# Expert pages of a top-1 MoE on one NeuronCore: token rows fetched as quarter rows and turned by VectorE instead of TensorE

## The chip, the cores and the metric

One core of a Trainium2 chip runs one launch of the kernel. The metric is the device time of that launch in microseconds (us), as the median of several runs. The engines are named as in the profile: PE (TensorE, matmuls and transposes), DVE (VectorE), ACT (ScalarE), POOL (GpSimd, here also the issuer of indirect DMAs) and SP (SyncE, the issuer of the plain DMAs).

## The reference

Sink-and-window attention (4 batches, 8 heads, 768 positions, head dimension 64), its output laid out as 3072 tokens of 512, then an FFN with `h * cos(h)`, then a mixture of 8 experts of which each token uses one. The change lies in the last part:

```python
def _moe2_ref(x, modality_id, w_gate, modality_bias, w1, w2):
    logits = x @ w_gate + modality_bias[modality_id]
    e_idx = np.argmax(logits, axis=1)
    probs = np.exp(logits - logits.max(-1, keepdims=True))
    probs /= probs.sum(-1, keepdims=True) + 1e-09
    gate_w = probs[np.arange(N), e_idx]
    for e in range(E):
        mask = e_idx == e
        h = np.maximum(x[mask] @ w1[e], 0.0)      # 512 -> 1024
        out[mask] = gate_w[mask, None] * (h @ w2[e])  # 1024 -> 512
    return out
```

Everything is float32. `x` here is the output of the FFN, one row of 512 for each token.

## The kernel before, in words

**Precision.** Each factor of a product is split into a high and a low part (`split`, L1096; `xh`, `xl`), and a product is three matmuls: high by high, high by low, low by high.

**Stages.** Attention and the FFN run first, woven into each other, in tiles of 384 tokens. `route_tile` computes a tile's gates and writes its rows to the DRAM scratch `y_scr`, 513 floats for each token: 512 of the row and the gate. It also counts where each token goes, and the table `inv` (128 by 192) ends with the token numbers in the order of the experts, a column for each half page.

**Pages.** The expert stage works on pages of 256 tokens of one expert. A page T passes through these steps:

- `gather_rows(T)` (L1116): six DVE operations of 128 by 2 turn two columns of `inv` into row numbers for the gather (`m_idg`) and for the scatter (`m_ids`). Both have four slots, T mod 4.
- `gather_go(T)` (L1128): two indirect DMAs on POOL's queue (L1131), each 128 rows of 513 floats, into `m_yg[T % 2]`. The token lies on the partition, so the row must be turned before it can be a factor of a product over the 512.
- `prelude(T)` (L1135): eight PE transposes of 128 by 128 (L1143) into PSUM, in two groups of four; after each group one copy on ACT (`xh`, L1144) and one subtraction on DVE (`xl`, by the helper at L149).
- `first_product` (L1147): 96 matmuls; ACT (L1154) and DVE (L146) make the two parts of `hT`.
- `second_product(T, h)`, for each half h: 48 matmuls, the copy `m_ot` on ACT with the gate as its scale (L1185), and the scatter of 128 rows to `out` on POOL's queue (L1188).

**Order.** From page 2 on a manual schedule holds: every engine runs its instructions in the order in which the code issues them. A full page T goes through the `If` branch of `run` (L1337): `first_product(T)`; then `ahead`: the load of the next expert's weights where the expert changes, `prelude(T+1)`, `second_product(T, 0)` with the splits of the next expert's first weights between its steps; then `gather_rows(T+2)`; then `second_product(T, 1)` with `gather_go(T+2)` between its copy and its scatter. A page of at most 128 tokens goes through the `Else` branch: it has half the work, and `gather_rows(T+2)` comes before `prelude(T+1)` there. Page 0 and the `prelude` of page 1 lie ahead of the manual schedule, woven into the end of the FFN.

**This input.** The run has pages 0 to 13. Pages 6 and 13 are half pages; the expert changes at page 6 and again at page 7, so that page 6 is the only page of its expert. In the profile page 2 starts at 850.80, page 6 at 946.1 and page 7 at 960.4 us.

Of the kernel before, what the change touches and what calls it, by code (L numbers as in the profile page):

```python
# [11 lines left out]
F32 = DT.float32  # L12
# [8 lines left out]
P = 128  # L21
# [41 lines left out]
def kernel(  # L63
# [634 lines left out]
    def ffn_tile_gen(ypool_of):  # L698
# [24 lines left out]
        for c in range(n_all + LAG):  # L723
# [28 lines left out]
            if c == n_all + LAG - 3:  # L752
                for r_ in routes:
                    for _ in r_:
                        pass
                routes.clear()
                ysb[NTILE] = [ypool_of().tile([P, YC], F32, name="yt", bufs=NQ) for _ in range(NQ)]
                for t in range(NQ):
                    SP.dma_start(out=ysb[NTILE][t][:, 0:DM], in_=yp_scr[t])
            i, f = seq[c - LAG] if c >= LAG else (0, -1)  # L760
            if f == span(i)[1] - 1:
# [6 lines left out]
                elif i == NTILE:  # L768
                    for t in range(NQ):
                        yt = ysb[i][t][:, 0:DM]  # L770
                        tt(DVE, yt, yps[i][t], yt, ALU.add)
                    ysb[0] = ysb.pop(NTILE)
                    routes.append(route_tile(0, ypool_of()))
                else:
                    ysb[i] = []
                    for t in range(NQ):
                        yt = ypool_of().tile([P, YC], F32, name="yt", bufs=NQ)
                        ACT.activation(out=yt[:, 0:DM], in_=yps[i][t], func=AF.Copy)
                        ysb[i].append(yt)
                    routes.append(route_tile(i, ypool_of()))  # L780
# [3 lines left out]
    def route_tile(i, yp):  # L784
# [284 lines left out]
    rw2 = fin.tile([P, KE, DM], F32, name="rw2")  # L1069
    m_yg = [[fin.tile([P, YC], F32, name=f"m_yg{i}{h}") for h in range(2)] for i in range(2)]  # L1070
    m_ix = [fin.tile([P, 2], F32, name=f"m_ix{i}") for i in range(4)]
# [17 lines left out]
    def load_raw(e, cond=None):  # L1089
        kw = {} if cond is None else dict(cond=cond, cond_hint=False)  # L1090
        for c in range(KD):
            SP.dma_start(out=rw1[:, c, :], in_=w1[ds(e, 1), c * P:(c + 1) * P, :].rearrange("o p f -> p (o f)"), **kw)
        for c in range(0, KE, 2):
            SP.dma_start(out=rw2[:, c:c + 2, :], in_=w2[ds(e, 1), c * P:(c + 2) * P, :].rearrange("o (c p) d -> p (o c) d", p=P), **kw)
# [16 lines left out]

    def gather(T, col, rows=NT):
        gather_rows(T, col)
        gather_go(T, rows)

# [11 lines left out]

    def gather_go(T, rows=NT):  # L1128
        idg = m_idg[T % 4]
        for h in range(2):  # L1130
            POOL.indirect_dma_start(out=m_yg[T % 2][h], out_offset=None, in_=y_scr[0:rows, :],  # L1131
                                    in_offset=bass.IndirectOffsetOnAxis(ap=idg[:, h:h + 1], axis=0),
                                    bounds_check=rows - 1, oob_is_err=False)

    def prelude(T, banks):  # L1135
# [40 lines left out]
    def second_product(T, h, yp, between=None, behind=None):  # L1176
        i = T % 2
        s = slice(h * P, (h + 1) * P)
        for f in range(KE):
# [3 lines left out]
            if between is not None:  # L1183
                between(f)
        ACT.activation(out=m_ot[h], in_=yp, func=AF.Copy, scale=m_yg[i][h][:, DM:YC])  # L1185
        if behind is not None:
# [12 lines left out]
    def lead():  # L1199
# [8 lines left out]
        load_raw(e0)  # L1208
        gather(0, e0 * NTI, NT - 2 * HALF)
        return e0  # L1210
# [14 lines left out]

    gather(1, e0 * NTI + 2)

# [113 lines left out]
    def run(T):  # L1341
# [39 lines left out]
        with tc.If(flags[T, "full"] > 0, preferred_fallthrough_block=True, label=f"full{T}" if T > 1 else None) as full:  # L1381
# [62 lines left out]
```

## Time and profile before

| | us |
|---|---|
| median of 3 runs | 1129.12 (1128.71 to 1129.29) |
| the profiled execution | 1130.26 |
| span of its profile | 1128.5 |
| busy: PE, PE weight loads | 1085.8 (96%), 917.2 (81%) |
| busy: DVE, ACT, POOL | 700.3 (62%), 607.9 (54%), 247.3 (22%) |

The span runs from the first to the last recorded instruction; the execution's own time has 1.76 us around it. A share of busy time is a mean over stages that differ: in the expert stage, from about 827 us on, DVE and ACT have little to do, and POOL issues DMAs alone. The chain that ended last is 82% PE, 6% DVE, 4% DMA and 3% ACT.

### The profile page before, as it was taken

The numbers are of one execution on the slowest core, as the hardware profiler recorded it, in microseconds if no ns is written. First come the engines' busy times: TensorE is split into PE (matmuls) and PEld (weight loads), VectorE is DVE, ScalarE is ACT, GpSimd is POOL, SyncE is SP. The second block draws the span as 40 slices with busy tenths as digits, with TensorE's granted clock in tenths as the row PEclk, the third lists the DMA queues.
The fourth block names the chain that finished last, engine by engine and source line by source line (L and its number), as shares of the span: only waits on it lengthen the run. The fifth ranks groups of instructions, "written<-read, shape, count | busy, mean of one in ns | idle before, by whom it ended". The sixth has DMA issues, their size and how long they took to land.

```text
span 1128.5 us, 20688 instructions
## 1 busy us (share of the span) xinstructions
PE 1085.8 (96%) x6432; PEld 917.2 (81%) x6432; DVE 700.3 (62%) x2186; ACT 607.9 (54%) x1243; POOL 247.3 (22%) x337
## 2 busy tenths in 40 slices
PE   5989999999999999999999999999999998999995
PEld 3667777788788888888888889899889997899984
DVE  6677888777977877886787674746731225522210
ACT  4879888665676666665766553334222225422221
POOL 1232233322212221222222211321112211221110
PEclk9989999999999999999999999999999999999998
DMA  6466675433332542433342132624151115111110
GB/s 152 134 187 181 199 232 147 102 83 83 89 91 68 111 89 65 101 75 82 74 107 68 56 114 73 254 64 114 47 188 58 58 40 188 39 59 40 40 41 24
DMA packets 171155, 113.38 MB, mean 100 GB/s; under 512 B 130799, under 2 KB 138991, under 8 KB 170992
## 3 DMA queue, kind: packets, MB, share of 16 engines
q1 hardware_dynamic: 166672, 97.88, 32.3%
q0 software_dynamic: 4320, 13.65, 3.7%
q8 instruction: 63, 1.03, 0.4%
q14 instruction: 100, 0.82, 0.2%
HBM read 151.06 MB, written 19.67 MB: 151 GB/s over the span
## 4 chain that ended last, share of the span: by engine, by line
PE 82%; DVE 6%; DMA 4%; ACT 3%; issue 2%; POOL 1%; SPq 0%; DVEq 0%; ACTq 0%; POOLq 0%
PE hp L137 21%; PE y L676 20%; PE m_y L137 11%; PE m_h L137 10%; PE ps L137 5%; PE po L137 5%; DMA out_dram<-m_ot,m_ids 3%; PE pl L804 1%; PE pt L589 1%; PE mh L137 1%; PE yT L793 1%; PE m_a L1143 1%; DMA cv_in<-in_moe_w_in_dram 1%; PE pt L588 1%; PE pz L626 1%
## 5 line engine op out<-in xcount | busy, mean ns | idle before, releaser
L149 POOL TENSOR_TENSOR g_l<-ch,g_h 128x384 fp32r<-128x384 f32 x128 | 133.6, 1044 | 471.6 <-ACT g_h L748 408.6
L137 PE MATMUL hp<-xT_h,wi_h 128*128 128x384 f32 x512 | 186.4, 364 | 2.2 <-DVE ch L149 2.2
L137 PE MATMUL hp<-xT_h,wi_l 128*128 128x384 f32 x512 | 175.1, 342 | 0.0
L137 PE MATMUL hp<-xT_l,wi_h 128*128 128x384 f32 x512 | 174.5, 341 | 0.0
L676 PE MATMUL y<-wo_l,g_h 128*128 128x512 f32 x384 | 155.7, 406 | 2.2 <-DMA wo_l<-wl_scr 2.2
L676 PE MATMUL y<-wo,g_h 128*128 128x512 f32 x384 | 156.9, 410 | 0.0
L676 PE MATMUL y<-wo,g_l 128*128 128x512 f32 x384 | 154.5, 402 | 0.2 <-POOL g_l L149 0.2
L738 ACT ACTIVATE ch<-ch,cols 128x384 f32<-128x384 f32 x128 | 78.7, 616 | 107.8 <-DVE ch L146 107.1
L137 PE MATMUL m_y<-wi_h,hT 128*128 128x512 f32 x416 | 132.5, 393 | 0.7 <-issue 0.5
L146 DVE SCALAR_TENSOR_TENSOR hT<-m_h,hT 128x256 fp32r<-128x256 f32 x88 | 37.4, 424 | 151.0 <-ACTq L1337 102.3
L137 PEld LDWEIGHTS hp<-xT_h,wi_h 128*128 128x128 f32 x512 | 96.9, 189 | 15.5 <-issue 4.5
L748 ACT ACTIVATE g_h<-ch 128x384 fp32r<-128x384 f32 x128 | 66.3, 520 | 69.7 <-DVE ch L149 46.2
L137 PEld LDWEIGHTS hp<-xT_l,wi_h 128*128 128x128 f32 x512 | 97.2, 190 | 4.4 <-issue 1.0
L143 DVE TENSOR_SCALAR ch<-hp 128x384 int32<-128x384 f32 x128 | 70.8, 553 | 46.6 <-PE hp L137 35.4
L137 PEld LDWEIGHTS hp<-xT_h,wi_l 128*128 128x128 f32 x512 | 96.8, 189 | 1.7 <-issue 1.4
L137 PEld LDWEIGHTS m_y<-wi_h,hT 128*128 128x128 f32 x416 | 78.1, 188 | 17.0 <-issue 0.9
L149 DVE TENSOR_TENSOR ch<-ch,hp 128x384 f32<-128x384 f32 x128 | 70.0, 547 | 29.7 <-ACT ch L738 29.2
L551 ACT ACTIVATE Pb<-Pb,mx 128x272 f32<-128x272 f32 (+1 forms) x168 | 82.8, 494 | 8.4 <-DVE mx L534 7.5
L676 PEld LDWEIGHTS y<-wo,g_l 128*128 128x128 f32 x384 | 72.3, 188 | 15.1 <-POOL g_l L149 1.0
L676 PEld LDWEIGHTS y<-wo,g_h 128*128 128x128 f32 x384 | 72.3, 188 | 13.9 <-issue 3.6
L676 PEld LDWEIGHTS y<-wo_l,g_h 128*128 128x128 f32 x384 | 72.5, 189 | 11.3 <-DMA wo_l<-wl_scr 2.5
L1154 ACT ACTIVATE hT<-m_h 128x256 fp32r<-128x256 f32 x88 | 34.0, 387 | 87.6 <-PE m_h L137 86.6
(289 smaller groups left out, 2288.8 us busy)
## 6 DMA issues: line engine op xcount, KB each, us to landing
rw<-in_moe_w_dram SPq DMA_DIRECT2D x112, 512.0 KB
wo_l<-wl_scr SPq DMA_DIRECT2D x122, 256.0 KB
cv_in<-in_moe_w_in_dram SPq DMA_DIRECT2D x16, 512.0 KB
cv_out<-in_moe_w_out_dram SPq DMA_DIRECT2D x16, 512.0 KB
y_scr<-yt SPq DMA_DIRECT2D x24, 256.5 KB
xT_h<-xg_h SPq DMA_DIRECT2D x32, 192.0 KB
xT_l<-xg_l SPq DMA_DIRECT2D x32, 192.0 KB
wl_scr<-wo_l SPq DMA_DIRECT2D x16, 256.0 KB
```

Of the source, the lines that this page charges most:

```text
L137: PE.matmul(o, l, r, start=start, stop=stop)
L143: e.tensor_scalar(out=o, in0=i, scalar1=s1, scalar2=s2, op0=op0, op1=op1)
L146: e.scalar_tensor_tensor(out=o, in0=i0, scalar=s, in1=i1, op0=op0, op1=op1)
L149: e.tensor_tensor(out=o, in0=a, in1=b, op=op)
L551: ACT.activation(out=Pb[t][j][:, c0:c1], in_=Pb[t][j][:, c0:c1], func=AF.Exp, scale=-1.0, bias=mx[:, i:i + 1], accum_out=sm[:, i:i + 1])
L588: PE.transpose(pt[:, j, 0:P], Pb[t][j][:, 0:P], ident)
L589: PE.transpose(pt[:, j, P:2 * P], Pb[t][j][:, SEG:W3], ident)
L626: PE.transpose(pz[0:nr, t * P:(t + 1) * P], pi_, ident)
L676: i = PE.matmul(o, l, r, start=start, stop=stop)
L738: ACT.activation(out=ch, in_=ch, func=AF.Sin, scale=TWO_PI, bias=half_pi)
L748: ACT.activation(out=gh, in_=ch, func=AF.Copy)
L1154: ACT.activation(out=hT_h[f], in_=hp, func=AF.Relu)
```

## The change

- **Scratch.** `y_scr` becomes a table of 12288 quarter rows of 128 floats, and the gates go to a scratch of their own, `g_scr`, by one more plain DMA for each tile. The three DVE copies for each tile that put the gate into column 513 go.
- **Quarter rows.** From page 2 on a page is fetched by eight indirect DMAs of 128 quarter rows (`gather_x`), such that the 32 partitions of group b hold quarter b of 32 tokens. The row numbers for it (`m_id8`) come from `inv4`, which holds the columns of `inv` four times, shuffled by `spread`: a cast on DVE, four matmuls on PE with the pattern `rep_t`, two copies on ACT, once, after page 1's gather. `gather_rows` gets two more DVE operations of 128 by 8.
- **Turning.** `prelude` for these pages has no PE transposes. Two DVE block transposes (each 32 by 32 within 128 by 512) go from `m_yg` to `m_xr` in SBUF, each followed by the copy on ACT and the subtraction on DVE. One `m_xr` group follows the other on DVE. The floats that one transpose reads are four apart, since the 512 are now dealt as (p c) over partition and chunk; the rows of `w1` are loaded in the same order.
- **Pages 0 and 1** keep whole rows and PE transposes, now with every fourth float as their operand.
- **Two pages ahead.** `gather_rows` and `gather_x` run in page T for page T+3. The gates of page T+2, two DMAs of 128 by 1, are fetched where the rows were.

```diff
@@ route_tile
         for t in range(NQ):
-            DVE.tensor_copy(ysb[i][t][:, DM:YC], gt[:, t:t + 1])
-            SP.dma_start(out=y_scr[(r0 + t) * P:(r0 + t + 1) * P, :], in_=ysb[i][t])
+            SP.dma_start(out=y_scr[(r0 + t) * P * KB:(r0 + t + 1) * P * KB, :].rearrange("(p c) y -> p (c y)", c=KB), in_=ysb[i][t])
+        SP.dma_start(out=g_scr[r0 * P:(r0 + NQ) * P, :].rearrange("(t p) o -> p (t o)", p=P), in_=gt)
@@ gather_rows
+        if T > 1:
+            id8 = m_id8[i]
+            ts(DVE, m_if.rearrange("p (h c) -> p h c", c=KB), inv4[:, ds(col, 2), :], -1.0, ALU.add, 0.0, ALU.max)
+            ts(DVE, id8, m_if, float(KB), ALU.mult, bq, ALU.add)
+    def gather_x(T):
+        yg = m_yg[T % 2]
+        if T > 1:
+            for c in range(2 * KB):
+                POOL.indirect_dma_start(out=yg[:, c * P:(c + 1) * P], out_offset=None, in_=y_scr[:, :],
+                                        in_offset=bass.IndirectOffsetOnAxis(ap=m_id8[T % 4][:, c:c + 1], axis=0),
+                                        bounds_check=NT * KB - 1, oob_is_err=False)
+    def spread():
+        DVE.tensor_copy(inv_r, inv[:, 0:NV])
+        for g in range(KB // 2):
+            pi = ps_a("spread")[:, 0:2 * NV].rearrange("p (c n) -> p c n", c=2)
+            for c in range(2):
+                mm(pi[:, c, :], rep_t[:, 2 * g + c, :], inv_r, True, True)
+            ACT.activation(out=inv4[:, 0:NV, 2 * g:2 * g + 2].rearrange("p n c -> p c n"), in_=pi, func=AF.Copy)
@@ prelude
         for g in range(KD // 2):
-            pt = banks[g].rearrange("p (c x) -> p c x", c=2)
-            for c in range(2):
-                for h in range(2):
-                    PE.transpose(pt[:, c, h * P:(h + 1) * P], yg[h][:, (2 * g + c) * P:(2 * g + c + 1) * P], ident)
+            if T < 2:
...
+            else:
+                pt = m_xr[:, 2 * g:2 * g + 2]
+                DVE.transpose(out=pt.rearrange("p k (c i) -> p k c i", i=TB),
+                              in_=yg.rearrange("p (c j k) -> p k c j", k=KD, j=TB)[:, 2 * g:2 * g + 2])
             ACT.activation(out=xh[g], in_=pt, func=AF.Copy)
             tt(DVE, xl[g], pt, xh[g].bitcast(F32), ALU.subtract)
@@ run
-        def rows_ahead():
+        def rows_ahead(step):
...
-            if T + 2 < NSUP:
-                with maybe(cond2):
-                    gather_rows(T + 2, val(3, T + 2, (ET.DVE,), NV - 1))
+            if T + 3 < NSUP:
+                with maybe(cond3):
+                    if step < 2:
+                        gather_rows(T + 3, val(3, T + 3, (ET.DVE,), NV - 1))
+                    if step > 0:
+                        gather_x(T + 3)
@@ run, full page
             ahead()
-            rows_ahead()
+            rows_ahead(1)
@@ run, Else
             look_ahead()
-            rows_ahead()
+            rows_ahead(0)
             ahead(after)
+            rows_ahead(2)
```

How this stands in the order of the engines. On POOL, page 1's full branch (pages 2 to 5 and 7 to 10 have the same pattern) held before, where `m_idg3` is page 3's row numbers and `m_ids1` page 1's:

```order
L1188 DMA out_0_dram<-m_ot0_8608,m_ids1_8597 3072x512
L1131 DMA m_yg10_8582<-y_scr_63,m_idg3_8595 128x513
L1131 DMA m_yg11_8583<-y_scr_63,m_idg3_8595 128x513
L1188 DMA out_0_dram<-m_ot1_8609,m_ids1_8597 3072x512
L1381 UNCONDITIONAL_BRANCH
```

and holds now, where `m_id80` is page 4's quarter row numbers and `m_gt1` page 3's gates:

```order
L1236 DMA out_0_dram<-m_ot0_8615,m_ids1_8604 3072x512
L1152 DMA m_yg0_8571<-y_scr_63,m_id80_8577 128x128 x8
L1165 DMA m_gt1_8574<-g_scr_64,m_idg3_8602 128x1 x2
L1236 DMA out_0_dram<-m_ot1_8616,m_ids1_8604 3072x512
L1441 UNCONDITIONAL_BRANCH
```

Eight quarter-row gathers for the page three ahead and two gate gathers stand between the page's two scatters, where two row gathers stood.

On DVE, the `Else` branch of page 6, between the end of its index work and the weight splits for page 7. Before, where `m_ids0` is page 8's scatter numbers and `m_x10`, `m_x11` the low parts of page 7:

```order
L149 TENSOR_TENSOR m_it0_8588<-m_it0_8588,m_ix0_8584 128x2 [waits DVE_49]
L143 TENSOR_SCALAR m_ix0_8584<-m_ix0_8584 128x2 [waits DVE_49]
L146 SCALAR_TENSOR_TENSOR m_ids0_8596<-m_it0_8588,m_ix0_8584 128x2 [waits DMASW6_49,DMASW7_49,DMASW4_49,DVE_49]
L149 TENSOR_TENSOR m_x10_8614<-m_a0_10050,m_x00_8612 128x512 [waits Activation_49]
L149 TENSOR_TENSOR m_x11_8615<-m_a1_10051,m_x01_8613 128x512 [waits Activation_49]
L1337 COMPARE_AND_BRANCH
L149 TENSOR_TENSOR wi_l0_88<-rw1_8578,wi_h0_78 128x512 [waits DMAHW1_49,Activation_49]
```

and now, where `m_ids1` is page 9's scatter numbers, a slot that page 5 used, and `m_yg1` holds page 7:

```order
L151 TENSOR_TENSOR m_it1_8596<-m_it1_8596,m_ix1_8592 128x2 [waits DVE_49]
L145 TENSOR_SCALAR m_ix1_8592<-m_ix1_8592 128x2 [waits DVE_49]
L148 SCALAR_TENSOR_TENSOR m_ids1_8604<-m_it1_8596,m_ix1_8592 128x2 [waits DMASW6_49,DMASW7_49,DMASW4_49,DVE_49]
L145 ISA
L145 TENSOR_SCALAR m_if_8576<-inv4_8589 128x8
L145 TENSOR_SCALAR m_id81_8578<-m_if_8576,bq_8581 128x8 [waits DVE_49]
L1190 STREAM_TRANSPOSE m_xr_8575<-m_yg1_8572 128x512 [waits DMASW2_49,DMASW5_49,DMASW1_49,DMASW0_49]
L151 TENSOR_TENSOR m_x10_8621<-m_xr_8575,m_x00_8619 128x512 [waits Activation_49]
L1190 STREAM_TRANSPOSE m_xr_8575<-m_yg1_8572 128x512
L151 TENSOR_TENSOR m_x11_8622<-m_xr_8575,m_x01_8620 128x512 [waits Activation_49]
L1391 COMPARE_AND_BRANCH
L151 TENSOR_TENSOR wi_l0_89<-rw1_8569,wi_h0_79 128x512 [waits DMAHW1_49,Activation_49]
```

The two block transposes stand ahead of the two subtractions' sources, one pair after the other; ahead of them now stand two more index operations, and the write of `m_ids` waits for DMAs of page 5's slot (`DMASW` are POOL's DMA semaphores) where it waited for page 4's.

## Rows read from the trace of the kernel before

**Rows 1.** Windows of the expert stage: start:end us, each engine's busy time, clock, DMA share, GB/s.

```profile
827.00:946.00 119.00, 116.82 (x761) 106.79 (x759) 33.61 (x90) 33.17 (x72) 21.38 (x21) 1.00 0.25 85
...
966.00:1104.00 138.00, 137.99 (x890) 126.12 (x891) 36.84 (x97) 35.18 (x76) 24.07 (x24) 1.00 0.15 47
```

**Rows 2.** Chain of waits, 780 to 1129 us: start us, length us, what.

```profile
812.43 0.35 PE pi L137 x2
...
839.02 0.87 PE m_a L1143 x8
839.89 10.91 PE m_y L137 x48
850.80 11.52 PE m_h L137 x96
...
954.24 0.87 PE m_a L1143 x8
...
1068.46 0.87 PE m_a L1143 x8
```

**Rows 3.** Groups by line, 800 to 1129 us, all engines: count | busy us, mean ns | idle.

```profile
L1143 PE MATMUL m_a<-ident,m_yg 128*128 128x128 f32 x104 | 13.5, 272 | 0.0
...
L149 DVE TENSOR_TENSOR m_x<-m_a,m_x 128x512 fp32r<-128x512 f32 x14 | 9.0, 686 | 4.1 <-ACT m_x L1144 4.0
...
L1144 ACT ACTIVATE m_x<-m_a 128x512 fp32r<-128x512 f32 x14 | 7.6, 596 | 5.3 <-PE m_a L1143 5.3
...
L146 DVE SCALAR_TENSOR_TENSOR m_ids<-m_it,m_ix 128x2 uint32<-128x2 f32 x13 | 2.1, 160 | 0.4
```

**Rows 4.** Groups by line with shapes apart, DVE, whole span: the block transpose.

```profile
L476 DVE STREAM_TRANSPOSE k_r<-kn 128x512 f32<-128x512 f32 x12 | 8.3, 690 | 0.0
```

**Rows 5.** The same view of DVE, 800 to 830 us: two operations of one size.

```profile
L141 DVE TENSOR_SCALAR tab<-g 128x20 f32<-128x20 f32 x1 | 0.2, 171 | 0.0
...
L141 DVE TENSOR_SCALAR tab<-page 128x20 f32<-128x20 f32 x1 | 0.2, 166 | 0.0
```

**Rows 6.** Timeline of DVE from 931 us, page 5: start us, us, engine, line, operation.

```profile
933.31 1.29 DVE L149 TENSOR_TENSOR m_xT_l<-m_a,m_xT_h 128x512 fp32r<-128x512 f32 x2 [0.18 <-ACT m_xT_h L1144]
934.52 4.90 DVE L149 TENSOR_TENSOR wi_l<-rw,wi_h 128x512 fp32r<-128x512 f32 x8
```

**Rows 7.** Timeline of DVE from 957.5 us, page 6 and start of page 7.

```profile
958.53 0.17 DVE L1120 COPY m_ix<-inv 128x2 f32 x1 [0.49 <-issue]
...
959.40 0.16 DVE L146 SCALAR_TENSOR_TENSOR m_ids<-m_it,m_ix 128x2 uint32<-128x2 f32 x1
959.48 1.28 DVE L149 TENSOR_TENSOR m_x<-m_a,m_x 128x512 fp32r<-128x512 f32 x2
960.68 4.90 DVE L149 TENSOR_TENSOR wi_l<-rw,wi_h 128x512 fp32r<-128x512 f32 x8
```

**Rows 8.** Timeline of PE from 959 us, the same place.

```profile
961.42 0.39 PE L137 MATMUL m_h<-m_x,wi_l 128*128 128x256 f32 x1 [0.59 <-DVE wi_l L149]
...
965.97 0.50 PE L137 MATMUL m_h<-m_x,wi_h 128*128 128x256 f32 x2 [0.70 <-DVE hT L146]
```

**Rows 9.** Timeline of POOL, 930 to 972 us: indirect DMAs as they are issued.

```profile
939.60 1.00 POOL L1188 DMA_INDIRECT out_dram<-m_ot,m_ids  x1 [15.57 <-DVE m_ix L1120]
940.90 1.05 POOL L1131 DMA_INDIRECT m_yg<-y_scr,m_idg  x1 [0.31 <-issue]
...
946.64 1.06 POOL L1188 DMA_INDIRECT out_dram<-m_ot,m_ids  x1 [0.65 <-DMA out_dram<-m_ot,m_ids]
963.69 2.80 POOL L1131 DMA_INDIRECT m_yg<-y_scr,m_idg  x1 [15.99 <-ACT m_ot L1185]
966.80 1.20 POOL L1131 DMA_INDIRECT m_yg<-y_scr,m_idg  x1 [0.31 <-issue]
```

**Rows 10.** DMA issues, 950 to 1120 us: count, KB each, median us to landing.

```profile
out_dram<-m_ot,m_ids POOLq DMA_INDIRECT x14, 3.0
```

**Rows 11.** The same view, 940 to 957 us, while an expert's weights load.

```profile
out_dram<-m_ot,m_ids POOLq DMA_INDIRECT x2, 6.2
```

More of the change, by code (lines that the diff above doesn't have):

```diff
@@ L756, in ffn_tile_gen @@
                 routes.clear()
-                ysb[NTILE] = [ypool_of().tile([P, YC], F32, name="yt", bufs=NQ) for _ in range(NQ)]
+                ysb[NTILE] = [ypool_of().tile([P, DM], F32, name="yt", bufs=NQ) for _ in range(NQ)]
                 for t in range(NQ):
-                    SP.dma_start(out=ysb[NTILE][t][:, 0:DM], in_=yp_scr[t])
+                    SP.dma_start(out=ysb[NTILE][t], in_=yp_scr[t])
             i, f = seq[c - LAG] if c >= LAG else (0, -1)
@@ L776, in ffn_tile_gen @@
                     for t in range(NQ):
-                        yt = ypool_of().tile([P, YC], F32, name="yt", bufs=NQ)
-                        ACT.activation(out=yt[:, 0:DM], in_=yps[i][t], func=AF.Copy)
+                        yt = ypool_of().tile([P, DM], F32, name="yt", bufs=NQ)
+                        ACT.activation(out=yt, in_=yps[i][t], func=AF.Copy)
                         ysb[i].append(yt)
@@ L1069 @@
     rw2 = fin.tile([P, KE, DM], F32, name="rw2")
-    m_yg = [[fin.tile([P, YC], F32, name=f"m_yg{i}{h}") for h in range(2)] for i in range(2)]
+    m_yg = [fin.tile([P, 2 * DM], F32, name=f"m_yg{i}") for i in range(2)]
+    m_gt = [fin.tile([P, 2], F32, name=f"m_gt{i}") for i in range(2)]
+    m_xr = fin.tile([P, KD, 256], F32, name="m_xr")
+    m_if = fin.tile([P, 8], F32, name="m_if")
+    m_id8 = [fin.tile([P, 8], U32, name=f"m_id8{i}") for i in range(4)]
+    bq = fin.tile([P, 1], F32, name="bq")
+    for b in range(KB):
+        POOL.memset(bq[b * TB:(b + 1) * TB], float(b))
+    rep_t = wpool.tile([P, KB, P], F32R, name="rep", tag=f"wo{KE + 6}")
+    POOL.tensor_copy(rep_t.rearrange("p c (b i) -> p c b i", i=TB),
+                     ident.rearrange("p (c i) -> p c i", i=TB).unsqueeze(2).to_broadcast([P, KB, KB, TB]))
+    inv_r = wpool.tile([P, NV], F32R, name="inv_r", tag=f"wo{KE + 7}")
+    inv4 = fin.tile([P, NV + 2, KB], F32, name="inv4")
+    POOL.memset(inv4[:, NV:], 0.0)
     m_ix = [fin.tile([P, 2], F32, name=f"m_ix{i}") for i in range(4)]
@@ L1110, in split_w2, with gather @@
         split(w2h[f], w2l[f], rw2[:, f, :], f)
-    def gather(T, col, rows=NT):
+    def gather(T, col, rows=NT, part=2):
         gather_rows(T, col)
-        gather_go(T, rows)
+        gather_go(T, rows, part)
     def gather_rows(T, col):
@@ L1139, in prelude @@
         for g in range(KD // 2):
[L1140 to L1143 removed]
+            if T < 2:
+                pt = banks[g].rearrange("p (c x) -> p c x", c=2)
+                for c in range(2):
+                    for h in range(2):
+                        PE.transpose(pt[:, c, h * P:(h + 1) * P],
+                                     yg[:, h * DM:(h + 1) * DM].rearrange("p (m k) -> p k m", k=KD)[:, 2 * g + c], ident)
+            else:
+                pt = m_xr[:, 2 * g:2 * g + 2]
+                DVE.transpose(out=pt.rearrange("p k (c i) -> p k c i", i=TB),
+                              in_=yg.rearrange("p (c j k) -> p k c j", k=KD, j=TB)[:, 2 * g:2 * g + 2])
             ACT.activation(out=xh[g], in_=pt, func=AF.Copy)
@@ L1184, in second_product @@
                 between(f)
-        ACT.activation(out=m_ot[h], in_=yp, func=AF.Copy, scale=m_yg[i][h][:, DM:YC])
+        ACT.activation(out=m_ot[h], in_=yp, func=AF.Copy, scale=m_gt[i][:, h:h + 1])
         if behind is not None:
@@ L1208, in lead @@
         load_raw(e0)
-        gather(0, e0 * NTI, NT - 2 * HALF)
+        gather(0, e0 * NTI, NT - 2 * HALF, 0)
         return e0
@@ L1224 @@
             pass
-    gather(1, e0 * NTI + 2)
+    gather(1, e0 * NTI + 2, NT, 0)
+    gather_go(0, NT, 1)
+    gather_go(1, NT, 1)
+    spread()
     s8 = [P, NE, NE]
@@ L1326 @@
         gather_rows(2, val(3, 2, (ET.DVE,), NV - 1))
+        gather_x(2)
+        gather_rows(3, val(3, 3, (ET.DVE,), NV - 1))
         second_product(0, 1, m_y[1], lambda f: prelude(1, m_a) if f == PPF else None, lambda: gather_go(2))
+        gather_x(3)
     m_h = [ps_h(f"m_h{i}") for i in range(2)]
```

32 lines of the change are left out of this document (21 added, 11 removed).

## Prediction

> **What bounds the kernel now.** I read the windows first, then the chain of waits, then DVE's and POOL's own timelines at the one place where PE stands still.
>
> In the windows [rows 1] PE is busy 116.82 of 119.00 us from page 1 to page 6, and 137.99 of 138.00 us from page 7 to page 13, at a granted clock of 1.00. DVE and ACT are each busy for about a quarter of that. So in these two stretches each microsecond taken from PE is a microsecond of the kernel, and work given to DVE and ACT costs nothing as long as it ends before PE asks for it.
>
> The chain [rows 2] shows what PE does for one page: 96 matmuls of the first product 11.52 us, the eight transposes of the next page's prelude 0.87 us, 48 matmuls of the second product 10.91 us: 23.30 us. The pieces "m_a L1143 x8" are what the change takes away. There are 12 preludes of pages 2 to 13. The group in [rows 3] has 104 transposes, 13 preludes of eight with page 1's.
>
> Between pages 6 and 7 the kernel is not bound by PE. Page 6 is a half page and the expert changes behind it, so DVE must finish there, one after another, the index work for page 8 (from 958.53), two subtractions for page 7 (1.28 us) and eight weight splits (4.90 us) [rows 7]; PE waits for splits from 961.42 on, and 0.70 us for DVE once more before 965.97 [rows 8]. Whatever lengthens DVE's work there lengthens the kernel.
>
> **The change, part by part.**
>
> *PE transposes of preludes.* Pages 2 to 13 lose 12 pieces of 0.87 us. The one before page 7 (954.24) is followed by DVE's chain, so its loss only lengthens PE's wait. 11 x 0.87 = **-9.57 us**.
>
> *What DVE does in their place.* A block transpose of 128 by 512 took 0.690 us [rows 4], a copy on ACT 0.60 and a subtraction 0.686 [rows 3]. One group of the new prelude waits for the other on DVE, and each subtraction waits for ACT: with hand-overs of a few hundredths, 2 x (0.69 + 0.66 + 0.69) = 4.08 us, where the two subtractions took 1.28. In a full page this lies beside the second product, 10.91 us [rows 2], and costs nothing. In page 5, where eight weight splits follow it, it starts near 933.2 and ends with them at 933.2 + 4.08 + 4.90 = 942.2 [rows 6], before the second product's end at 944.0 (933.08 + 10.91). Without that cover each prelude would cost 4.08 us.
>
> *Page 7.* Here there is no cover. DVE's chain grows by 4.08 - 1.28 = **+2.80 us**, and by two more index operations, some 0.2 us each with their hand-over: **+0.40 us**. The third term is a new wait. `gather_rows` for page 9 runs here now, and its `m_ids` slot is page 5's, so DVE waits until page 5's second scatter has landed. On POOL that scatter now stands behind eight quarter gathers and two gate gathers, which can start only when page 5's index work, behind its weight splits, is done: 942.2 + 0.95 + 0.40 = 943.5. Indirect DMAs leave POOL 1.31 us apart (939.60 and 1.00 + 0.31 [rows 9]), so the scatter is issued at 943.5 + 10 x 1.31 = 956.6. At a landing time of 3.0 us [rows 10] it is down at 959.6. DVE reaches `m_ids` at 959.40, and 0.87 us earlier against page 5's clock (prelude of page 6), at 958.5. Wait: **+1.1 us**. While an expert's weights load, scatters landed in 6.2 us [rows 11]; with that the wait is 4.3 us. I take 1.1, because the scatter would leave when those loads are over or nearly so, and keep 0 to 4.3. Behind the waiting instruction on DVE stand the transposes, the subtractions, the splits and, through them, PE. Page 7 in sum: **+4.3 us**.
>
> *Strided reads on DVE.* The new transposes read every fourth float, 16 bytes apart. The trace has one pair of like size: 0.171 us for an operand 32 bytes apart and 0.166 for a dense one [rows 5]. That is nearly no difference, though on 20 elements only; I take the dense duration. The other bound: the smallest operations take 0.160 us [rows 3], so 0.53 of the 0.69 go with the elements; doubled, a transpose takes 1.22 us. That is +1.06 us at page 7 and nothing elsewhere. [...]
>
> *Strided operands of PE.* Pages 0 and 1 keep 16 transposes, now with floats 16 bytes apart. No row shows such a weight load. Taken as 0; twice the pace is the other bound, +0.87 for each prelude, +1.74.
>
> *Spread.* Four matmuls of 128 by 192 (two took 0.35 us [rows 2]) are 0.7 us on PE, where PE has no gap; with a wait for the cast, **+0.9 us**. The two copies are ACT's. `inv4` is first needed for page 2's numbers, several microseconds later.
>
> *POOL.* A full page now issues 12 DMAs, not 4: 12 x 1.31 = 15.7 us of a page of 23.30 - 0.87 = 22.43 us. It fits, and costs nothing. Page 3's last quarter gather stands behind all of page 1's: 15.7 us after that page's first half result, near 845.2, so 860.9, landing 863.9 to 867.1 by 3.0 and 6.2. DVE then needs 4.08 us, to 871.2 at most, and page 3 starts at 839.02 + 10.91 + 11.52 + 10.91 = 872.4. Taken as 0, at most 1.
>
> *Two pages ahead.* A full page's own gather was hidden before and is hidden now: no gain. *Gates apart:* one more plain DMA for each tile and three DVE copies fewer, in a region where attention and FFN set the time: 0. *w1 rows in another order:* the same bytes in pieces as long as before: 0.
>
> **Sum:** -9.57 + 2.80 + 0.40 + 1.1 + 0.9 = -4.4 us, rounded to -4.3 for the hand-overs. The profiled execution took 1130.26 (span 1128.5), so it would take 1126.0. It lies 1.14 us above the median of the runs, 1129.12; against that the forecast is **1124.8 us**, 0.4% less. A measurement of this kernel tells about 0.2%, 2.3 us, from no change.
>
> **Rivals.**
>
> *A. Nothing much is left (no change).* Page 7 eats the gain: strided transposes (+1.06), strided weight loads (+1.74), and the scatter landing late (up to +3.2 beyond my 1.1). Two of the three suffice. For it: the DMA engines carry weights up to about 957, and the scatter leaves then. Against it: [rows 5]. -4.3 + 1.06 + 1.74 + 1.5 = 0.0: **1129.1 us**.
>
> *B. No wait for the scatter.* Issue is faster or page 6 longer than I think. Then the sum is -5.5: **1123.6 us**; if the ACT copies overlap the transposes better too, up to -7.5, 1121.6.
>
> *C. POOL becomes the bound (slower).* Place: POOL's queue between a page's two scatters. Price: p us from one indirect DMA to the next. The wait at page 7 is 1.1 + 10 x (p - 1.31), so the gain is gone at p = 1.75, and from p = 22.43 / 12 = 1.87 on every page with 12 DMAs is bound by POOL. At p = 2.0 page 7's wait is 8.0, the sum +2.5, and 1.6 us come on top for each of some nine pages: 1131.6 to **1146 us**. For it: one gather took 2.80 us while DVE ran weight splits [rows 9, 7]. Against it: another took 1.06 us at 946.64, and the pace elsewhere is 1.31. [...]
>
> *D. It doesn't do what it says:* the transposes stay on PE's path because PE waits for DVE at each page. That needs a prelude of over 10.91 us on DVE, more than twice what I count; I give it no chance of its own.
>
> **How the numbers follow.** Forecast 0.47; A 0.25; B 0.15; C 0.13. Forecast and B lie below 1126.9, the bound of 0.2%: faster 0.62. A: same 0.25. C: slower 0.13. The range reaches from B's far half, 1121.5, to the forecast with all upper bounds (-4.3 + 1.06 + 1.74 + 3.2 = +1.7), 1130.8. It leaves out C and the edges of A and B.
>
> **What would show it.** A page of 22.43 us in the chain, no "m_a" pieces in it, eight of them left for page 1 alone: the first term. DVE's transposes at 0.69 us, not 1.22. POOL's indirect DMAs at 1.31 us. A wait of DVE for a scatter at `m_ids` in page 6, of about 1 us, and page 7's first full run of matmuls some 4.3 us later against page 6's start. PE without a wait at the starts of pages 2 to 6 and 8 to 13. I am wrong if pages of 23 us or more remain, if DVE waits at page 7 for over 4 us, or if PE waits for a prelude at any full page.

## The result, and the profile after

The changed kernel takes **1134.91 us** (median of 8 runs, 1130.63 to 1138.41); the kernel before, run beside it, 1128.58 (8 runs, 1125.42 to 1129.29). The ratio is 1.0058 with an interval of 1.0041 to 1.0075: slower by 0.6%. The forecast was 1124.8 in a range of 1121.5 to 1130.8, so both the direction and the range were wrong. The profiled execution of the changed kernel took 1135.09, 4.83 more than the one of before, where the forecast had 4.3 less. On another chip the same kernel took 1244 us, and on a third its variants took some 1235; that has a section of its own below. The experiments ran on a chip on which it takes 1135 us again, called the first chip here, unless the text names another.

The page of the changed kernel, span and busy time:

```profile
span 1133.1 us, 20853 instructions
...
PE 1078.6 (95%) x6340; PEld 910.1 (80%) x6340; DVE 726.4 (64%) x2211; ACT 610.8 (54%) x1245; POOL 350.4 (31%) x443
```

PE has 7.2 us less to do than before and the kernel ends later: PE waits more. The chain of waits of the changed kernel shows that the gain is there (compare [rows 2]):

```profile
994.53 11.51 PE m_h L139 x96
1006.05 10.91 PE m_y L139 x48
1016.96 11.51 PE m_h L139 x96
```

A page is 22.43 us long, 0.87 less, with no transposes in it. Its groups by line, 800 to 1134 us, answer to [rows 3] and [rows 4]:

```profile
L1152 POOL DMA_INDIRECT m_yg<-y_scr,m_id x96 | 98.2, 1023 | 40.0 <-issue 27.1 <-DVE m_id L145 11.4 <-DMA m_yg<-y_scr,m_id 1.2
...
L1190 DVE STREAM_TRANSPOSE m_xr<-m_yg 128x512 f32<-128x512 f32 x24 | 25.9, 1078 | 3.7 <-DMA m_yg<-y_scr,m_id 3.6
...
L148 DVE SCALAR_TENSOR_TENSOR m_ids<-m_it,m_ix 128x2 uint32<-128x2 f32 x13 | 2.1, 165 | 5.7 <-DMA out_dram<-m_ot,m_ids 5.0 <-DVE m_ix L145 0.4
```

The block transpose takes 1.078 us, not 0.690, and DVE waited 5.0 us in all for a scatter at `m_ids`. Where the time went can be read from PE's timelines, by the start of each page's first product, one profile of each kernel (for page 2 of the kernel before, the chain's 850.80 in [rows 2] starts a little later than the timeline's 850.6):

| start of page | 1 | 2 | 3 | 4 | 6 | 7 | 8 | 13 |
|---|---|---|---|---|---|---|---|---|
| before | 826.9 | 850.6 | 873.9 | 897.2 | 946.1 | 960.4 | 986.7 | 1103.6 |
| changed | 831.7 | 854.5 | 876.9 | 900.2 | 945.1 | 968.7 | 994.4 | 1107.7 |

Two places lose what the pages gain: the stretch ahead of page 1 (4.8 us), and page 6 to page 7 (14.3 us before, 23.6 now).

**Ahead of page 1.** At 290 us the changed kernel is 0.3 us ahead of the kernel before (from 80 to 200 us it was some 2 us ahead). Then its PE stops, for DVE:

```profile
295.70 0.33 PE L139 MATMUL hp<-xT_h,wi_l 128*128 128x384 f32 x1
298.55 0.30 PE L581 MATMUL pt<-ident,Pb 128*128 128x128 f32 x1 [2.52 <-DVE Pb L143]
```

DVE in turn stood before an attention transpose whose input was late:

```profile
294.45 0.16 DVE L560 RECIPROCAL sm<-sm 128x2 f32<-128x2 f32 x1
297.58 0.58 DVE L464 STREAM_TRANSPOSE q_r<-qn 128x384 f32<-128x384 f32 x1 [2.97 <-DMA qn<-in_q_dram]
```

and on SP's queue the write of the gates stands right ahead of that load:

```profile
287.70 0.38 SPq L836 DMA_DIRECT2D g_scr<-rgt  x1
288.13 0.49 SPq L439 DMA_DIRECT2D qn<-in_q_dram  x1
...
291.66 5.68 SPq L453 DMA_DIRECT2D vs_n<-in_v_dram  x3
```

A tile's 384 gates lie one for each partition and token group, so the write is 384 pieces of 4 bytes. The windows of that place, first before, then changed (columns as in [rows 1]):

```profile
290.00:300.00 10.00, 9.95 (x54) 8.42 (x53) 9.63 (x46) 7.67 (x13) 1.43 (x2) 1.00 0.57 144
```

```profile
290.00:300.00 10.00, 7.48 (x40) 6.30 (x39) 6.79 (x35) 6.83 (x11) 1.01 (x1) 0.97 0.60 56
300.00:310.00 10.00, 10.00 (x55) 8.23 (x54) 8.68 (x25) 2.67 (x5) 2.31 (x5) 0.86 0.34 71
```

The DMA engines are busy for the same share and move 56 GB/s instead of 144. After its stop PE is granted a clock of 0.86 in the mean of the next 10 us, where the kernel before has 1.00. The changed kernel, 0.3 us ahead at 290 us, is 3.6 us behind at 305 us and 2.7 from 320 us on, so that the stop of 2.5 us costs 3.0. A second, smaller loss (1.1 us) lies near 728 us, and 1.4 us more are lost between 806 us and page 1, where `spread` takes 0.4 us of PE.

**Page 7.** DVE in page 6 of the changed kernel, answering to [rows 7]:

```profile
958.37 0.17 DVE L145 TENSOR_SCALAR m_ix<-m_ix 128x2 f32<-128x2 f32 x1
963.52 0.16 DVE L148 SCALAR_TENSOR_TENSOR m_ids<-m_it,m_ix 128x2 uint32<-128x2 f32 x1 [4.99 <-DMA out_dram<-m_ot,m_ids]
...
964.03 1.08 DVE L1190 STREAM_TRANSPOSE m_xr<-m_yg 128x512 f32<-128x512 f32 x1
965.80 0.69 DVE L151 TENSOR_TENSOR m_x<-m_xr,m_x 128x512 fp32r<-128x512 f32 x1 [0.70 <-ACT m_x L1192]
966.41 1.07 DVE L1190 STREAM_TRANSPOSE m_xr<-m_yg 128x512 f32<-128x512 f32 x1
968.17 0.69 DVE L151 TENSOR_TENSOR m_x<-m_xr,m_x 128x512 fp32r<-128x512 f32 x1 [0.70 <-ACT m_x L1192]
968.78 4.90 DVE L151 TENSOR_TENSOR wi_l<-rw,wi_h 128x512 fp32r<-128x512 f32 x8
```

The wait that I had foreseen is there, 4.99 us long. The scatter that ends it is the last row of POOL's queue, answering to [rows 9]:

```profile
946.60 1.04 POOL L1152 DMA_INDIRECT m_yg<-y_scr,m_id  x1 [0.85 <-DVE m_id L145]
...
950.56 1.49 POOL L1152 DMA_INDIRECT m_yg<-y_scr,m_id  x1 [0.30 <-issue]
952.36 1.50 POOL L1152 DMA_INDIRECT m_yg<-y_scr,m_id  x1 [0.30 <-issue]
954.17 1.00 POOL L1152 DMA_INDIRECT m_yg<-y_scr,m_id  x1 [0.30 <-issue]
...
960.68 1.03 POOL L1236 DMA_INDIRECT out_dram<-m_ot,m_ids  x1 [0.30 <-issue]
```

Ten DMAs from 946.60 on, the scatter at 960.68, on the ground at 963.40 (2.72 us in the chain of waits). PE runs out of work at 958.67 and stands still until page 7's first weights are split:

```profile
968.71 0.79 PE L139 MATMUL m_h<-m_x,wi_h 128*128 128x256 f32 x2 [10.04 <-ACT wi_h L1112]
```

It starts again at a granted clock of 0.50:

```profile
970.00:975.00 5.00, 5.00 (x25) 5.00 (x25) 5.00 (x10) 4.48 (x10) 1.55 (x2) 0.50 0.01 3
```

**Page 3** loses 1 us more: POOL waits for the gates of the last tile until 819.18, from there on issues DMA after DMA with pauses of 0.30 to 0.31 us, and reaches that page's last quarter gather at 867.90; the serial prelude behind it ends after PE wants it (DVE, then PE):

```profile
870.63 1.09 DVE L1190 STREAM_TRANSPOSE m_xr<-m_yg 128x512 f32<-128x512 f32 x1 [3.56 <-DMA m_yg<-y_scr,m_id]
```

```profile
877.79 0.39 PE L139 MATMUL m_h<-m_x,wi_l 128*128 128x256 f32 x1 [0.52 <-DVE m_ix L1135]
```

### The profile page after: what moved, and what is told of

The parts are those of the page before. It is cut to its first block, busy times and chain, and to the rows that moved or that the text cites. A ratio compares the mean times of both kernels' runs of the same rounds, so it can differ in the third digit from the quotient of the medians.

```text
span 1133.1 us, 20853 instructions
## 1 busy us (share of the span) xinstructions
PE 1078.6 (95%) x6340; PEld 910.1 (80%) x6340; DVE 726.4 (64%) x2211; ACT 610.8 (54%) x1245; POOL 350.4 (31%) x443
## 5 line engine op out<-in xcount | busy, mean ns | idle before, releaser
L1152 POOL DMA_INDIRECT m_yg<-y_scr,m_id x96 | 98.2, 1023 | 40.0 <-issue 27.1
L151 DVE TENSOR_TENSOR ch<-ch,hp 128x384 f32<-128x384 f32 x128 | 70.0, 547 | 26.9 <-ACT ch L740 26.3
L678 PEld LDWEIGHTS y<-wo,g_h 128*128 128x128 f32 x384 | 72.3, 188 | 14.3 <-issue 3.6
L139 PE MATMUL m_h<-m_x,wi_h 128*128 128x256 f32 x384 | 72.5, 290 | 10.2 <-ACT wi_h L1112 10.0
```

The costliest lines, as they stand in the source:

```text
L139: PE.matmul(o, l, r, start=start, stop=stop)
L151: e.tensor_tensor(out=o, in0=a, in1=b, op=op)
L678: i = PE.matmul(o, l, r, start=start, stop=stop)
L1152: POOL.indirect_dma_start(out=yg[:, c * P:(c + 1) * P], out_offset=None, in_=y_scr[:, :], in_offset=bass.IndirectOffsetOnAxis(ap=m_id8[T % ...
```

## The experiments

The theory: the transposes' gain is real and whole; it is lost to three things that can each be taken away alone, the gate write in 4-byte pieces, the wait at `m_ids` for an old scatter, and the long serial chain of strided transposes. The rivals: that POOL's pace makes the loss (rival C of the prediction), and that the loss ahead of page 1 is a matter of the order of instructions there, with the gates no part of it. Times of before stand in brackets, from the same chip and the same set of runs.

### Six slots for the scatter numbers

```diff
-    m_ids = [fin.tile([P, 2], U32, name=f"m_ids{i}") for i in range(4)]
+    m_ids = [fin.tile([P, 2], U32, name=f"m_ids{i}") for i in range(6)]
-        ix, it, idg, ids = m_ix[i], m_it[i], m_idg[i], m_ids[i]
+        ix, it, idg, ids = m_ix[i], m_it[i], m_idg[i], m_ids[T % 6]
```

> The changed kernel with six slots for m_ids instead of four, so that gather_rows(9) in page 6 no longer writes the slot that page 5's second scatter reads. Theory (DVE's wait for that scatter, 4.99 us, is what holds page 7): the wait goes, DVE's prelude for page 7 starts near 958.6 instead of 964.0, page 7's first product ends 4 to 5 us earlier, the median falls from 1134.9 to about 1130. Rival (the weights of page 7's expert, loaded until about 960, or ACT's splits would hold page 7 anyway): less than 2 us, 1133 or more.

Measured: 1129.99 (1129.33), ratio 1.0005 [0.9991, 1.0020], 4.9 us less than the changed kernel. DVE runs through:

```profile
960.16 0.16 DVE L148 SCALAR_TENSOR_TENSOR m_ids<-m_it,m_ix 128x2 uint32<-128x2 f32 x1
...
961.06 1.08 DVE L1190 STREAM_TRANSPOSE m_xr<-m_yg 128x512 f32<-128x512 f32 x1
```

Page 6 to page 7 takes 19.1 us instead of 23.6. POOL issues the same ten DMAs at the same pace (14.10 us), and DVE no longer waits for the scatter behind them. So it is the reused slot that makes the wait, and POOL's queue only sets how long it is. Rival C, which makes POOL's pace the bound, falls here too.

### The gates written as three long pieces

```diff
-        SP.dma_start(out=g_scr[...].rearrange("(t p) o -> p (t o)", p=P), in_=gt)
+        PE.transpose(pr_[0:NQ, P:2 * P], gt, ident)
+        grow = yp.tile([NQ, P], F32, name="rgrow")
+        ACT.activation(out=grow, in_=pr_[0:NQ, P:2 * P], func=AF.Copy)
+        SP.dma_start(out=g_scr[...].rearrange("(t p) o -> t (p o)", p=P), in_=grow)
```

> The changed kernel, but each tile's gates are turned by one PE transpose and written to g_scr as 3 pieces of 512 bytes instead of 384 pieces of 4 bytes. Theory (the 384 small pieces hold up loads of the attention behind them on the DMA queues: DVE waited 2.97 us for a q tile right after the first such write): the loss of 3 us ahead of page 1 goes, page 1's first product starts near 828 instead of 831.7, the median is about 1132. Rival (the loss is the clock or the other weave of attention and FFN): page 1 starts at 831 or later, the median stays at 1134 to 1135.

Measured: 1129.59 (1129.33), ratio 1.0000 [0.9988, 1.0013]. By medians that is 5.3 us less than the changed kernel; by the two profiled executions, of which this one was the slowest of its twelve, 1.4. In the trace page 1 starts at 828.4 instead of 831.7. This start differs by up to 3.7 us from one execution of the same instructions to the next, so more than one profile counts. With the small pieces (the changed kernel twice, six slots, both transposes first) it lies at 831.7, 832.8, 833.2 and 834.7, with the long ones (this run and all three together) at 828.4 and 824.6, and in two profiles of the kernel before at 826.9 and 826.6. The stop near 299 us is gone:

```profile
290.00:300.00 10.00, 10.00 (x57) 8.56 (x57) 9.73 (x41) 9.31 (x19) 1.10 (x1) 1.00 0.29 65
```

The write also sits elsewhere in SP's order now, at 297.83 behind that tile's attention loads. This run alone doesn't tell the small pieces from their place in the queue; the next one bears on that.

### The gate write alone, added to the kernel before

The kernel before, with the same write of 384 pieces to a scratch that nothing reads.

```diff
+    g_scr = dram.tile([NT, 1], F32, name="g_scr")
+        SP.dma_start(out=g_scr[r0 * P:(r0 + NQ) * P, :].rearrange("(t p) o -> p (t o)", p=P), in_=gt)
```

> The kernel before with one thing added: each tile's gates are also written to a scratch g_scr of their own, in 384 pieces of 4 bytes, which nothing reads. Theory (the small pieces hold up the attention's loads): PE stands still for 2 to 3 us near 299 us, the clock falls for a while after it, and the median rises by 3 to 4 us, to 1132 to 1133. Rival (the other weave of the attention, not the write): no such stop, 1129.

> The kernel of e6 (the one before, with gates also written in 4-byte pieces) once more, as it too was in that run, 14 us slower with its loss between 700 and 842 us. Theory of the small pieces as told for e2: 1132 to 1134. If the code of e6 itself costs 14 us: 1143 again.

> The kernel before with gates also written in 4-byte pieces. On a chip where the changed kernel takes 1135: by the theory of the small pieces 1132 to 1133, with PE standing still near 299 us; by its rival 1129. Where the changed kernel takes 1240: 1144 as before, and no verdict.

Measured on three chips: 1144.65 (1129.87) on the first, 1143.46 (1129.55) and 1144.52 (1130.54) on the second and third. On the first chip the ratio is 1.0123 [1.0099, 1.0147], 14.8 us. The expectation was right in sign and far off in size and place: there is no stop near 299 us. In this kernel four of the eight writes cost next to nothing. Behind the other four PE falls back, on the first chip by 4.8 us near 584 us, 4.9 near 724, 5.4 near 800 and 3.7 near 831 (on the other two chips the first of these is missing). At the first three PE waits for loads of `wo_l`, at the last for something that the profile calls remote. Near 800 us the write stands ahead of `y_scr`'s rows and of a load of `wo_l`. SP there, then PE there and near 724:

```profile
785.95 0.37 SPq L836 DMA_DIRECT2D g_scr<-rgt  x1
786.41 1.41 SPq L835 DMA_DIRECT2D y_scr<-yt  x3
787.91 0.41 SPq L722 DMA_DIRECT2D wo_l<-wl_scr  x1
```

```profile
723.98 0.50 PE L677 MATMUL y<-wo_l,g_h 128*128 128x512 f32 x1 [2.05 <-DMA wo_l<-wl_scr]
...
802.58 0.80 PE L677 MATMUL y<-wo_l,g_h 128*128 128x512 f32 x1 [4.12 <-DMA wo_l<-wl_scr]
```

The windows around 800 us and at the last place, with the write and (second fence) before:

```profile
780.00:800.00 20.00, 18.45 (x97) 16.35 (x95) 16.06 (x53) 9.98 (x16) 5.08 (x5) 1.00 0.73 69
820.00:830.00 10.00, 8.33 (x59) 7.31 (x58) 7.17 (x49) 1.58 (x5) 0.00 (x0) 1.00 0.93 51
```

```profile
780.00:800.00 20.00, 19.81 (x110) 17.38 (x108) 14.60 (x33) 6.59 (x12) 4.48 (x4) 1.00 0.41 102
820.00:830.00 10.00, 9.29 (x55) 7.69 (x54) 3.77 (x14) 2.81 (x5) 3.68 (x4) 1.00 0.65 216
```

So behind 1.5 KB in pieces of 4 bytes the DMA engines were busy 0.73 and 0.93 of the time at 69 and 51 GB/s, and loads of `wo_l` behind such writes came late (PE waited 2.05 and 4.12 us for them). Page 1 starts 17 us later, and the expert pages are as long as before. Not each such write cost time: from 290 to 300 us the DMA engines of this kernel are busy 0.98 of the time, and PE loses nothing. That it is costly holds in both kernels (14.8 us here, 5.3 in the changed one), and here the order of instructions can hardly be blamed: on PE, DVE, ACT and POOL it is the same as before, and on SP, besides the eight writes, two loads of `wo_l` change places.

### Dense reads for the transposes

The features are dealt so that a block reads 32 floats in a row; `w1` comes in 16 loads of 32 rows, and ACT makes two more copies for each of pages 0 and 1.

```diff
-                              in_=yg.rearrange("p (c j k) -> p k c j", k=KD, j=TB)[:, 2 * g:2 * g + 2])
+                              in_=yg.rearrange("p (c k j) -> p k c j", k=KD, j=TB)[:, 2 * g:2 * g + 2])
```

> The changed kernel with another dealing of the 512 over partition and chunk, so that the two block transposes read runs of 32 floats; w1 is loaded to match in 16 pieces of 32 rows, and pages 0 and 1 get two extra copies on ACT ahead of their PE transposes. Theory (16-byte steps make the transposes slow): a transpose takes 0.69 us instead of 1.08, page 5's and page 7's preludes are 0.8 us shorter each, the median falls by 1 to 1.6 us, to about 1133.5. Rival (they are slow for another reason, such as POOL's DMAs at the same time): 1.0 us or more each, no change.

Measured: 1144.87 (1129.33), ratio 1.0130 [1.0108, 1.0152]. The transposes do what was disputed:

```profile
L1195 DVE STREAM_TRANSPOSE m_xr<-m_yg 128x512 f32<-128x512 f32 x24 | 16.9, 706 | 0.2
```

0.706 us for the same work with dense reads, against 1.078. The total is spoiled by my own additions: the ACT copies for page 1 wait for its gather at the head of ACT's queue, and PE stands behind them, so that page 1 starts at 840.9:

```profile
829.72 0.79 PE L139 MATMUL m_y<-wi_h,hT 128*128 128x512 f32 x1 [5.42 <-ACT hT L1207]
```

At page 7 the chain from the first transpose to the splits is 4.03 us, where it was 4.75. But there the scatter leaves while weights still load (the DMA engines are busy 0.77 of the time from 968 to 974 us) and lands some 5.7 us later, DVE waits 6.57 us at `m_ids`, and page 6 to page 7 takes 25.3 us. As a way to win the 0.37 us it is a failure; as a price of the stride it stands.

### Both transposes first

```diff
+        for g in range(KD // 2) if T > 1 else ():
+            DVE.transpose(out=m_xr[:, 2 * g:2 * g + 2]..., in_=yg...)
         for g in range(KD // 2):
...
-                DVE.transpose(...)
```

> The changed kernel with both block transposes of a prelude ahead of both subtractions. Theory (in page 7 and in page 5 the prelude's serial chain on DVE and ACT is on the path): the chain from the first transpose to the end of the last subtraction falls from 4.8 to about 3.6 us, page 7 gains 1.2 us there and up to 1.2 more as page 5's index work, and so its second scatter, is earlier; the median is about 1132.5 to 1133.7. Rival (the scatter's landing alone sets page 7): the wait grows by what the chain loses, no change.

Measured: 1131.93 (1129.33), ratio 1.0018 [1.0005, 1.0032], 3.0 us less than the changed kernel. ACT's first copy now runs beside the second transpose:

```profile
964.71 0.16 DVE L148 SCALAR_TENSOR_TENSOR m_ids<-m_it,m_ix 128x2 uint32<-128x2 f32 x1 [4.69 <-DMA out_dram<-m_ot,m_ids]
...
965.21 2.05 DVE L1182 STREAM_TRANSPOSE m_xr<-m_yg 128x512 f32<-128x512 f32 x2
967.19 1.47 DVE L151 TENSOR_TENSOR m_x<-m_xr,m_x 128x512 fp32r<-128x512 f32 x2
968.57 4.90 DVE L151 TENSOR_TENSOR wi_l<-rw,wi_h 128x512 fp32r<-128x512 f32 x8
```

From the first transpose to the splits 3.36 us, where it was 4.75, although the wait at `m_ids` is still there. Page 6 to page 7 takes 21.4 us. Page 3 runs without PE's wait, as it does with dense reads, so its loss needs the long chain.

### All three

Six slots, long pieces for the gates, both transposes first.

> Six slots, both transposes first and gates turned by PE together, once more. On a chip where the changed kernel takes 1135: theory (three separate losses) 1123.5, rival (they share one wait) 1127 or more. Where the changed kernel takes 1240: 1240 here as well, and no verdict.

Measured: **1121.47** (1129.87), ratio 0.9933 [0.9918, 0.9947]: 13.7 us less than the changed kernel (1135.19 in the same set), where the three alone gave 4.9, 5.3 and 3.0, together 13.2. So the losses are separate and add up, as far as the medians tell it (the interval of each ratio is some 1.6 us to either side). The traces say the same of page 6 to page 7: 23.6 us in both profiles of the changed kernel, 4.5 less with six slots, 2.3 less with both transposes first, 7.0 less with all three. The three-part version beats both kernels. Page 1 starts at 824.6, page 6 at 938.0, page 7 at 954.6, and PE's wait at page 7 is down from 10.04:

```profile
954.64 0.80 PE L139 MATMUL m_h<-m_x,wi_h 128*128 128x256 f32 x2 [4.01 <-ACT wi_h L1115]
```

In that set the kernel before and the changed kernel were measured again as kernels of their own:

> The kernel before, unchanged, run as a kernel of its own. In two jobs the changed kernel and its variants took 100 us more than in two others, with all engines standing still in the expert stage for work that the profile does not show. If this comes with the chip or with how a program lies there, this may show it too (over 1140); if it needs the changed kernel's many indirect DMAs, this is at 1129.

> The changed kernel for the third time, as the control of the chip of this job: 1135 on a chip like the first, 1240 on one like the other.

1128.83, ratio 0.9997 [0.9985, 1.0010], and 1135.19, ratio 1.0050 [1.0030, 1.0070].

### Two other chips, where the times give no verdict

Three more variants were meant to tell POOL's order from the slot: the gathers behind the page's second scatter; in the `Else` branch all work for the page ahead behind the prelude; and that together with the long gate pieces and both transposes first.

```diff
-            rows_ahead(1)
+            rows_ahead(0)
             look_ahead()
             second_product(T, 1, m_y[1], None, after)
+            rows_ahead(2)
```

```diff
-            rows_ahead(0)
             ahead(after)
-            rows_ahead(2)
+            rows_ahead(1)
```

> The changed kernel with the eight quarter-row gathers of a full page issued behind the page's second scatter instead of ahead of it; slots as in the changed kernel. Theory (the scatter that DVE waits for is late because it stands behind eight gathers that wait for page 5's index work): page 5's second scatter is issued at about 948 instead of 960.7, DVE's wait at m_ids in page 6 is gone, page 7's first product ends 4 to 5 us earlier, the median is near 1130, as with six slots. Rival (the landing is slow because the weights load at the time, whenever the scatter leaves): a wait of 2 us or more stays, 1132 or more.

> The changed kernel with one move in the branch for half pages: gather_rows for the page three ahead comes behind prelude(T+1) and the first half of the second product, as in full pages, and not ahead of them (its row numbers are not needed there any more). Theory (in page 6 the index work and its wait for a scatter stand ahead of page 7's prelude on DVE, and all of that is on the path): page 7's first product ends 6 us earlier, 5.0 for the wait and 1.3 for eight small operations; the median is about 1128.6, some 1.4 below six slots. Rival (what follows on DVE then waits for the weights of page 7's expert): no better than six slots, 1130.

> The changed kernel with three of these together: gates turned by PE and written in 512-byte pieces, both transposes ahead of both subtractions, gather_rows behind the prelude in half pages. Theory (the three losses are separate and add): 5.3 + 1.2 + 6.3 = 12.8 us below the changed kernel, about 1122, 0.6% below the kernel before. Rival (they share one wait, or the next one is close behind): 1125 or more.

They ran on a second chip and took 1234.55, 1236.16 and 1233.89 (1129.55). The times give no verdict, but the trace of the first shows what the order does:

```profile
1008.24 1.55 POOL L1236 DMA_INDIRECT out_dram<-m_ot,m_ids  x1 [0.30 <-issue]
```

This is page 5's second scatter, 3.7 us after the start of page 6 (1004.56); in the changed kernel it left 15.6 us after it (960.68 against 945.09). DVE comes to `m_ids` some 13.5 us after that start in both, and here it doesn't wait. So the wait has two conditions, the reused slot and the place of the old scatter behind the ten DMAs.

A third chip was then given the changed kernel itself, with one of these variants and the three-part version:

> The changed kernel itself once more, as the control of e5, e7 and c1, which took some 100 us more: all engines stood still in every page with nothing in the profile that released them. If that came with the chip or the loading of a program, this may be at 1230 too; if it came with the code, this is at 1135, with a page of 22.4 us.

> The kernel of e7 once more, beside the changed kernel. If the code is the cause: 1236 again, with pages of 32 us. If the loading is: about 1128.6, as expected for it first, with page 7's first product 6 us earlier than in the changed kernel.

> The changed kernel with six slots for m_ids, both transposes ahead of both subtractions and the gates turned by PE, each of which alone took about 1130, 1132 and 1130. Theory (three separate losses): 4.9 + 1.2 + 5.3 below 1134.9, about 1123.5, 0.5% below the kernel before. Rival (they share one wait): 1127 or more.

1244.03, 1235.62 and 1241.99 (1130.54). So it needs no variant: the changed kernel is 10% slower than the kernel before on the third chip and 0.5 to 0.6% slower in two other sets of runs, one of them on the first chip, and the kernel before takes the same time on all three. On the third chip most full pages take 30 to 34 us instead of 22.43, in the stretches in which POOL issues indirect DMAs; there PE waits for nothing that the profile shows, ACT for something that it calls remote, while POOL keeps its pace. ACT, PE and POOL of the changed kernel on the third chip:

```profile
919.33 0.38 ACT L1202 ACTIVATE hT<-m_h 128x256 fp32r<-128x256 f32 x1 [6.08 <-remote]
```

```profile
920.22 0.80 PE L139 MATMUL m_h<-m_x,wi_h 128*128 128x256 f32 x2 [4.38 <-issue]
```

```profile
917.32 1.00 POOL L1165 DMA_INDIRECT m_gt<-g_scr,m_idg  x1 [0.30 <-issue]
918.62 1.03 POOL L1236 DMA_INDIRECT out_dram<-m_ot,m_ids  x1 [0.30 <-issue]
```

What differs stays open; each of the two slow chips served a single set of runs, so that chip and set can't be told apart. The three-part version's gain holds for the first chip alone.

## Why the prediction was wrong, point by point

| us, against the profiled execution of before | predicted | measured |
|---|---|---|
| 11 preludes off PE | -9.57 | -9.57 |
| ahead of page 1 (`spread`, gates) | +0.9 | +4.8 |
| page 3 | 0 | +1.0 |
| start of page 6 | 0 | -2.1 |
| page 6 to page 7 | +4.3 | +9.3 |
| start of page 13 | 0 | +0.8 |
| rest | 0 | +0.6 |
| sum | -4.3 | +4.8 |

The first measured row is 0.87 us for each of 11 pages. The rows of the starts of pages 6 and 13 are PE's idle time there, before and after; the others are differences of the page starts, and the rest is what they leave of 4.83.

- **Preludes: right.** Pages of 22.43 us, eight transposes left for page 1 alone, full pages but page 3 hide the new prelude.
- **"Gates apart: one more plain DMA for each tile and three DVE copies fewer ... 0": the largest miss.** I counted the DMA as one issue and its bytes as few. It is 384 pieces, and the load behind it on SP's queue came late (DVE waited 2.97 us for it). So a term that I had put at 0 because attention and FFN set the time there cost 5.3 us by medians, which is what the long pieces give back. Whether `spread` took its 0.9 isn't shown: PE is busy with it for 0.4 us, and with the gates repaired page 1 starts 1.5 us later than before in one profile and 2.3 earlier in another.
- **"Wait: +1.1 us" at `m_ids`: right mechanism, wrong size, 4.99.** Counted from the start of page 5, the scatter was to land after 39.1 us (959.6 - 920.5) and landed after 40.7 (963.40 - 922.7): 0.8 us are the two slower transposes ahead of page 8's index work, 1.0 is POOL's ten DMAs in 14.08 us, not 13.1, and a landing in 2.72 gives 0.3 back. DVE was to be there after 38.0 and was after 35.8 (958.5 - 922.7), because PE no longer stood still at the start of page 6. 1.1 + 1.6 + 2.2 = 4.9. The 2.1 us won at the start of page 6 were luck, since no step of mine forecast them, and they were only waited for later. My upper bound of 4.3 was 0.7 short.
- **"I take the dense duration": wrong.** The short pair of [rows 5] did not carry to 128 by 512: 1.078, between the dense 0.69 and the doubled 1.22. The chain grew by 3.55 (4.75 - 1.20) where I had 2.80. The doubling behind 1.22, +1.06 us in rival A and in the range, was an assumption that no run shows: with the stride a transpose took 0.37 us more (1.078 against 0.706 in the dense run), 0.74 for the two of page 7.
- **Page 3, "taken as 0, at most 1": the bound was met** (0.96 with its hand-overs), but barely, and not in the run with the long gate pieces (1.9). Both transposes first takes the wait away, so the longer chain is part of it. POOL's late start behind the gates (it waited 19.36 us for `g_scr`) does not explain it: with the long pieces POOL begins at 810.04, 9.1 us earlier, and page 3 loses more. What delays the last gather there stays open.
- **Right, at a cost of nothing:** strided operands of PE (282 ns for a transpose against 272), POOL's pace outside the weight splits (1.30 to 1.31), the rest of a page's POOL work.
- **The rivals.** C is refuted as a bound by POOL's pace, which it wanted at 1.75 us or more: the ten DMAs in page 6 leave 1.41 apart. That 1134.9 lies in its range of 1131.6 to 1146 is luck. The two gathers of 1.49 and 1.50 us were issued while DVE ran weight splits, a third, at 949.26, took 1.00 beside them: such gathers were together at most 1.0 us longer here (0.49 + 0.50 above 1.00). A had the right place (page 7 eats the gain) and two of its three causes in part. No rival named the gate write; with it repaired the change would have made no difference (1.0000).
- **Left open:** PE stands 2.11 us at the start of page 6 before and not at all after (a second profile of each shows 2.21 and nothing), and 0.81 at the start of page 13 after and not before. Both are entries to the branch for half pages. What moved it was not tried.

## What to carry to other kernels

Count a DMA by its pieces, not by its bytes or its issues alone: here eight writes of 1.5 KB, each in 384 pieces of 4 bytes, cost 14.8 us when they were added to the kernel before, and turning the gates into rows first gave 5.3 us back in the changed one. When a step is moved earlier, look for the older reader of each buffer slot that it writes (here page 5's second scatter, a wait of 4.99 us); place that reader on its own queue, in the new order, before sizing the wait, or give the slot more depth (six slots gave 4.9 us back). Where nothing covers a chain, put both long operations first, so that the other engine's part runs beside the second (3.36 us here instead of 4.75).

## What the runs showed that I had not expected

- A block transpose of 128 by 512 floats took 1.078 us with its reads 16 bytes apart and 0.706 with runs of 32 floats.
- With the gate writes of 384 pieces of 4 bytes the DMA engines were busy 0.73 of the time from 780 to 800 us and 0.93 from 820 to 830, at 69 and 51 GB/s, where the kernel before had 0.41 and 0.65 at 102 and 216.
- One kernel took 1135 us on one chip and 1244 on another, while the kernel before took 1129 to 1131 on both.
- After PE's stop of 10 us ahead of page 7 the granted clock was 0.50 from 970 to 975 us: three matmuls took 0.64 us instead of 0.36. PE had no idle time in that page, which took 25.7 us; before, at a clock of 1.00 and with waits for DVE's splits, it took 26.3.
